# Normalizing the late attention runs through TensorE in a two-layer attention and mixer kernel

## The chip, the cores and the metric

The kernel runs on one core of one Trainium2 chip. The metric is the device time of one launch in microseconds (us). Times of several runs are given as a median; durations of single instructions come from one profiled execution.

The engines go by the profile's names: PE is TensorE (matmuls; PEld its weight loads), DVE is VectorE, ACT is ScalarE, POOL is GpSimd, SP is the engine whose queue issues most DMAs.

## The reference

Two blocks alternate, twice each, on x of 2048 tokens by 640 features (bf16 inputs):

```python
x = x + attention(layernorm(x), wqkv, wo)       # 32 heads of 20
x = x + token_mlp(layernorm(x), w1, b1, w2, b2) # over the 2048 tokens, 1536 hidden
x = x + attention(layernorm(x), wqkv, wo)
x = x + token_mlp(layernorm(x), w1, b1, w2, b2)

def attention(x, wqkv, wo):
    q, k, v = heads(x @ wqkv)
    p = softmax(q @ k.T * 20 ** -0.5)
    return merge(p @ v) @ wo

def token_mlp(x, w1, b1, w2, b2):      # x is normalized once more here
    u = gelu(layernorm(x).T @ w1 + b1)
    return (u @ w2 + b2).T
```

The scores are 32 x 2048 x 2048 per layer, so the work of attention is 134 million exponentials per layer.

## The kernel before, in words

**Attention.** Heads are taken four at a time (a group g of 8, each head padded to 32 partitions). A *unit* is one block of 512 queries (qb, four of them), one group and one tile of 128 keys (kt); it holds four *chunks* of 128 x 512 scores, one per head. For a chunk, PE makes S (128 keys x 512 queries, line L703), ACT turns three or two chunks at a time into P with one exponential (L773, 1536 or 1024 wide, alternating), and PE adds P times V into the accumulator `acc` (L1326). V has a column of ones per head, so row 20 of each head's 32 rows of `acc` is the softmax's sum. The sixteen units of one block and group are a *run*. In the last block of queries the units are 256 queries wide, and the last run is split in two halves.

Part of the chunks is not exponentiated on ACT but on DVE and POOL, in pairs, by integer and polynomial steps (L563, L661, L593, L597, L644, L614 or L616), from a PSUM bank `Dt` of their own into tiles `Pd`.

**Normalization of a run** (`finish_run`), all on DVE: `turn` transposes `acc` in 32 x 32 blocks into the f32 tile T1 (L810), so that queries come to lie on partitions; `recip` inverts the sums (L823); `scaled` multiplies (L826, into the bf16 tile T2); `back` transposes again into `attnT` (L834), which feeds the output projection. There is one accumulator bank: the next run's first product with V waits until `turn` has read it.

**Fills.** Everything else that PE does in attention is a *fill*, a short series of products into one PSUM bank (`misc`; early on also `Dt`), followed by an evacuation on DVE or ACT: the transposes of normalized tokens (T, L1225), projections to K and Q (L1177) and V (L1201), the output projection (O, L1117 and L1155), the first product of the mixer (M: six or eight products with `w1st`, L1068, added to the rows `ua` at L1076, whose weights come by DMA into two buffers), and in layer 1 the second product of layer 0's mixer (y, L1685).

**Order.** The order of all engines' work is written out while the program is built, by a planner that keeps a clock for each engine: `emit_S`, `emit_exp` and `emit_PV` lay out the main work, and `slot_work` puts fills into the gaps between the S products of two exponentials, in the order of a priority (`add_fill`). A fill's cost and its share of PE's activity are numbers that the caller states. [...] DVE's work is a list of `Proc`s, each with a rank and a list of steps with their costs. At the ramp of a layer, K and Q of the first groups are made as their tokens arrive: blocks of 512 tokens (tb), groups 0 to 3, for query blocks 0 and 1.

**End of a layer's attention.** After the last exponential, the planner runs what is left of the fills (`fill_step(tail_alloc)`) while the last run is normalized; `end_tiles` then makes the output projection of the last two token tiles in the S banks (L960), runs the remaining fills, whose evacuations are collected in `held`, and normalizes the two tiles: statistics (L980, `gather`), the rest (`spread`) and the apply steps (L995 on ACT, L999 on DVE). Then filler products keep PE going until the mixer's first products (`um`, L1753) of `mixer_head`. After layer 0 the mixer's head is followed by layer 1's ramp, after layer 1 by the mixer's tail (L1766, L1825).

Before the change the banks for these last fills are taken from a list of three:

```python
tail_banks = [sums[0][:, 1024:1536], None, None]

def tail_alloc():
    bank = tail_banks.pop()
    return bank if bank is not None else Dbank.alloc() if len(tail_banks) == 1 else misc.alloc()
```

At the very start, on DVE, the ones of V's extra column are set by a memset (L1546) among the statistics of the first token tiles.

Of the kernel before, what the change touches and what calls it, by code (L numbers as in the profile page):

```python
# [13 lines left out]
F32 = mybir.dt.float32  # L14
# [54 lines left out]

HOLD = 3  # L70
WARM_WAVES = 14
LOG2E = 1.4426950408889634
# [9 lines left out]
def kernel(  # L82
# [61 lines left out]
    ident = consts.tile([128, 128], BF16, name="ident")  # L144
    make_identity(nc, ident[:])
    mhalf = consts.tile([128, 1], F32, name="mhalf")
    nc.vector.memset(mhalf[:], -0.5)
# [76 lines left out]
    def attention(st, x_in_ap, x_mid, uacc_l, feed, feed_stack):  # L224
# [505 lines left out]
        def zeros(t):  # L730
            acc = runs[pv_run[0]]["acc"] if pv_run[0] < len(runs) else None
            if acc is not None:
                bank = acc
            elif not s_start:
                bank = warm_bank()
            elif late and fs["cur"] is not None and fs["idx"] > 0:
                zero_wave(fs["tile"], False, False, fs["cur"]["wave"], 512 if fs["cur"]["wave"] == WAVE else 320)
                return True
            elif fs["cur"] is None and misc.free <= pem["t"]:
                bank = misc.alloc()  # L740
            elif late and Dbank.free <= pem["t"]:
                bank = Dbank.alloc()
            elif t + 1 in S_tiles and pem["t"] + (0.0 if pem["mode"] == "S" else TURN) + PE_TO_ACT < exp_end.get(t, 0.0):
                for i, (n, j) in enumerate(tiles[t + 1]):
                    s_matmul(S_tiles[t + 1][:, i, :], n, j)
                s_start[t + 1] = pe_wave("S", cells=0.25 * len(tiles[t + 1]))
                return True
            else:
                return False
            zero_wave(bank, acc is None, acc is None)  # L750
            return True
# [39 lines left out]
        def finish_run(run):  # L791
# [8 lines left out]
            nth = part_no.get((qb, g), 0)  # L800
            whole = run["final"]
            if not whole:
                part_no[(qb, g)] = nth + 1

            def turn(end):
                if not whole and nth == 0:
                    box["T1"] = part_view((qb, g))
                else:
                    box["T1"] = ntmp.tile([128, 512], F32, name="T1")[:, c0:c1]
                nc.vector.transpose(out=box["T1"], in_=acc[:, c0:c1])  # L810
                acc_free[0] = end + DVE_TO_PE
# [16 lines left out]

            def back(end):
# [3 lines left out]
                to = attnT_tiles[qb][g]  # L833
                nc.vector.transpose(out=to[:, c0:c1], in_=T2[:, 0:nb, :].rearrange("p c i -> p (c i)"))  # L834

# [10 lines left out]
            rest = [(0.5, added, 0.0, True)] if nth else []  # L846
            if whole:
                rest += [(0.244, recip, 0.0), (0.15 + 0.34 * part, scaled, 0.0, True), (0.15 + 0.56 * part, back, 0.0)]
            ahead = [p for p in dvm["procs"] if getattr(p, "norm", False)]
            first = Proc(0, [(0.15 + 0.56 * part, turn, 0.0)], at + PE_TO_DVE)  # L850

            def turned(end):
                if rest:
                    p = Proc(norm_rank(run), rest, end + DVE_NEXT, after=after if whole else None,
                             allow=lambda me: not whole or (bool(late) and (len(me.steps) > 1 or at_live[0] < NG + 4)))
                    p.norm = True
                    submit(p)
            first.after = turned
            first.allow = lambda me: not any(p in dvm["procs"] for p in ahead)
            submit(first)  # L860

        early_left = set(early_runs)
        at_live = [0]
# [353 lines left out]
        def t_fill(tt, h_bf, ready, done):  # L1217
# [15 lines left out]
            def after(end):  # L1233
# [3 lines left out]
                if all(4 * tb + i in tready for i in range(4)):  # L1237
# [9 lines left out]
                    if tb in EQ and tb > 0:  # L1247
                        for g in range(EG):
                            proj_fill("Q", g, tb, base[tb] + 16.0 + 8.0 * g - 4, at, fed=True)
                if len(tready) == NT and NQB > 1:  # L1250
# [202 lines left out]
        for t in sums:  # L1453
            zero_wave(t[:, 0:512], True, True)
            zero_wave(t[:, 512:D], True, True, HALF / 2, D - 512)
        tail_banks = [sums[0][:, 1024:1536], None, None]

        def tail_alloc():
            bank = tail_banks.pop()
            return bank if bank is not None else Dbank.alloc() if len(tail_banks) == 1 else misc.alloc()  # L1460
        room = pem["t"] + 1.3
# [9 lines left out]
    class TokenFeed:  # L1471
        groups = 4
        early_qbs = (0, 1)
        ve_early = True
        act_helps = True
        act_free = 0.0
# [22 lines left out]
        def after_end(self, cx):  # L1499
            nc.gpsimd.memset(wo_pad[:], 0.0)  # L1500
            setup_wo()
            setup_biases()
# [3 lines left out]
        def begin(self, cx):  # L1506
# [376 lines left out]
```

## Time and profile before

| | |
|---|---|
| median of 3 runs | 1754.15 us (1754.06 to 1754.17) |
| the profiled execution's own time | 1754.05 us |
| its span, first to last instruction | 1752.3 us |
| mean granted TensorE clock | 1.000 |
| first exponential starts | 15.97 us |
| last exponential of layer 0 ends; first `um` product | 816.82; 823.27 us |
| first exponential of layer 1 starts | 853.26 us |
| last exponential of layer 1 ends; first `um` product | 1681.39; 1689.30 us |

A line of a group reads: source line, engine, operation, out<-in by tile names, shapes, count, then busy us, mean ns of one, then the engine's idle time just before them and what ended it. A line of a timeline reads: start, duration, engine, line, operation, count, and in brackets the idle time before it and what ended that. Line numbers are those of the kernel before.

### The profile page before, as it was taken

Reading aid. Unit: us, or ns where it says so; the run is one execution under the profiler, and the core shown is the slowest. Engines: PE = TensorE matmul, PEld = TensorE weight load, DVE = VectorE, ACT = ScalarE, POOL = GpSimd, SP = SyncE. Lnnn points to the kernel's source line nnn. Section 1 sums busy time; section 2 is a strip of 40 time slices with the busy share of each in tenths; the row PEclk is TensorE's granted clock in tenths of the full one; section 3 lists DMA queues with packets and bytes.
Section 4 is the critical chain, followed back from the end, with each engine's and each line's share of the span. In section 5 each row is a group of like instructions: output and inputs, shape, how many; then the busy total and the mean of one; then the engine's idle time right before and its main releaser. Section 6 shows DMA issues by size and latency. Waiting matters only on the chain.

```text
span 1752.3 us, 43289 instructions
## 1 busy us (share of the span) xinstructions
PE 1677.7 (96%) x17891; PEld 663.4 (38%) x17891; DVE 1534.9 (88%) x2491; ACT 1665.0 (95%) x1498; POOL 592.0 (34%) x936
## 2 busy tenths in 40 slices
PE   8999999999999999999999999999999999999999
PEld 3333333333333344444434433233333333444455
DVE  7789999999999999998543469999999999999973
ACT  8999999999999999999779999999999999999970
POOL 2243443353544343332000023434434443434310
PEclk9999999999999999999999999999999999999999
DMA  4020000000122010133322100001001220101445
GB/s 117 9 24 10 1 2 2 24 24 2 35 66 82 25 47 3 39 97 97 125 69 75 65 11 1 1 2 43 20 2 61 82 76 6 62 3 40 120 122 178
DMA packets 103014, 81.87 MB, mean 47 GB/s; under 512 B 50976, under 2 KB 87456, under 8 KB 102816
## 3 DMA queue, kind: packets, MB, share of 16 engines
q1 hardware_dynamic: 97280, 71.22, 13.5%
q0 software_dynamic: 5536, 7.88, 1.5%
q8 instruction: 140, 2.29, 0.5%
q14 instruction: 58, 0.48, 0.1%
HBM read 55.48 MB, written 23.59 MB: 45 GB/s over the span
## 4 chain that ended last, share of the span: by engine, by line
ACT 50%; PE 25%; issue 22%; DVE 2%; DMA 1%; POOL 0%; SPq 0%; ACTq 0%; DVEq 0%
ACT P L773 50%; PE S L703 7%; PE acc L1326 4%; PE misc L1068 2%; PE ya L1766 2%; PE misc L1177 2%; PE acc L762 2%; PE um L1753 1%; PE Dt L1177 1%; PE ya L1775 1%; PE yb L1766 1%; DMA w2s<-in_B_w_dram 1%; PE misc L1117 0%; PE misc L1685 0%; PE misc L1201 0%
## 5 line engine op out<-in xcount | busy, mean ns | idle before, releaser
L773 ACT ACTIVATE P<-S 128x1536 bf16<-128x1536 f32 (+1 forms) x1430 | 1617.4, 1369 | 13.5 <-PE S L703 13.0
L703 PE MATMUL S<-QTq,KT 32*128 32x512 bf16 (+1 forms) x4449 | 575.6, 337 | 60.9 <-ACT P L773 44.4
L661 POOL TENSOR_SCALAR ey<-ew 128x512 f16<-128x512 uint16 x516 | 320.6, 621 | 689.6 <-DVE et L597 306.4
L703 PEld LDWEIGHTS <-KT 32*128 32x128 bf16 x5127 | 229.6, 91 | 524.6 <-issue 497.0
L563 DVE TENSOR_SCALAR ew<-Dt 128x512 int32<-128x512 f32 x524 | 357.0, 681 | 22.3 <-PE Dt L703 14.8
L1326 PE MATMUL acc<-P,Vaug 128*32 128x512 bf16 (+1 forms) x4442 | 363.3, 343 | 0.3 <-DVE Vaug L370 0.3
L762 PE MATMUL acc<-zr,zw 128*32 128x512 bf16 x4256 | 328.1, 382 | 1.2 <-POOL zr L155 1.2
L597 DVE SCALAR_TENSOR_TENSOR et<-ey,ew 128x1024 int16<-128x1024 f16 x262 | 325.6, 1243 | 2.8
L644 POOL TENSOR_SCALAR Pd<-ew 128x512 int16<-128x512 int16 x317 | 196.8, 627 | 161.6 <-DVE et L597 42.4
L703 PE MATMUL Dt<-QTq,KT 32*128 32x512 bf16 (+1 forms) x678 | 201.4, 333 | 0.0
L593 DVE TENSOR_TENSOR ey<-ey 128x1024 f16<-128x1024 f16 x262 | 188.3, 719 | 1.4 <-POOL ey L661 0.3
L1326 PEld LDWEIGHTS <-Vaug 128*32 128x32 bf16 x5120 | 102.7, 94 | 175.4 <-issue 161.4
L762 PEld LDWEIGHTS <-zw 128*32 128x32 bf16 x4476 | 111.5, 96 | 97.9 <-issue 52.5
L616 DVE SCALAR_TENSOR_TENSOR Pd<-ew,et 128x1024 int16<-128x1024 int16 (+1 forms) x134 | 134.6, 1005 | 0.6
L614 DVE TENSOR_TENSOR Pd<-Pd,et 128x1024 int16<-128x1024 int16 (+1 forms) x189 | 121.8, 645 | 5.8 <-POOL Pd L644 3.8
L903 POOL TENSOR_TENSOR rstd<-veps,mhalf 128x1 f32<-128x1 f32 x60 | 49.4, 824 | 224.6 <-DVE veps L901 197.2
L1326 PE MATMUL acc<-Pd,Vaug 128*32 128x512 bf16 (+1 forms) x678 | 102.9, 336 | 1.4 <-DVE Pd L614 1.2
L1177 PE MATMUL misc<-hh,wq_pad 128*128 128x512 bf16 x290 | 84.0, 383 | 0.0
L1068 PEld LDWEIGHTS <-w1st 128*128 128x128 bf16 x672 | 52.9, 97 | 58.2 <-issue 45.3
L1177 PE MATMUL misc<-hh,wk_pad 128*128 128x512 bf16 x255 | 74.0, 383 | 0.0
L1068 PE MATMUL misc<-x1last,w1st 128*128 128x320 bf16 x384 | 73.0, 302 | 0.0
L1117 PE MATMUL misc<-wo_pad,attnT 128*128 128x320 bf16 x384 | 72.3, 302 | 0.2 <-DVE xin L1129 0.2
(145 smaller groups left out, 1180.4 us busy)
## 6 DMA issues: line engine op xcount, KB each, us to landing
w2s<-in_B_w_dram SPq DMA_DIRECT2D x16, 768.0 KB
uacc<-ustg POOLq DMA_DIRECT2D x24, 320.0 KB, 2.6
x1in<-xd SPq DMA_DIRECT2D x24, 320.0 KB
w1st<-in_B_w_dram SPq DMA_DIRECT2D x24, 256.0 KB
xd<-x2s SPq DMA_DIRECT2D x16, 320.0 KB
xin<-xd SPq DMA_DIRECT2D x16, 320.0 KB
w1st<-in_B_w_dram SPq DMA_DIRECT2D x24, 192.0 KB
xd<-x1s SPq DMA_DIRECT2D x12, 320.0 KB
```

The source lines that it names most:

```text
L563: nc.vector.tensor_scalar(out=w[:, slot, :], in0=Dt[:, :], scalar1=127.0 * FIX, scalar2=0.0, op0=ALU.add, op1=ALU.max)
L593: nc.vector.tensor_tensor(out=y, in0=y, in1=y, op=ALU.mult)
L597: nc.vector.scalar_tensor_tensor(out=box["t"][:, 0:512 * k], in0=ve_y.pop(p)[:, 0:512 * k], scalar=MANT_C * MANT_K ** 2, in1=frac, op0=ALU ...
L616: nc.vector.scalar_tensor_tensor(out=bits, in0=whole[:, lo:hi], scalar=128.0, in1=t, op0=ALU.mult, op1=ALU.add)
L644: after_vector(nc.gpsimd.tensor_scalar(out=bits, in0=whole, scalar1=128.0, scalar2=0.0, op0=ALU.mult, op1=ALU.add))
L661: return engine.tensor_scalar(out=out_ap, in0=in_ap, scalar1=MANT_K / FIX, scalar2=-MANT_K * MANT_S, op0=ALU.mult, op1=ALU.add)
L703: pe(nc.tensor.matmul(out_ap[:, c0:c0 + w], lhsT=KT[32 * j:32 * j + 32, g, kt * 128:(kt + 1) * 128], rhs=get_QT(st, qb)[32 * j:32 * j + 32 ...
L762: pe(nc.tensor.matmul(bank[32 * j:32 * j + 32, 0:w], lhsT=zw[:], rhs=zr[:, :, 0:64].to_broadcast([128, w // 64, 64]), start=start, stop=st ...
L773: nc.scalar.activation(out=P[:, 0:ncs, :].rearrange("p a b -> p (a b)"), in_=St[:, 0:ncs, :].rearrange("p a b -> p (a b)"), func=ACT.Exp, ...
L1068: pe(nc.tensor.matmul(t[:, 0:w], lhsT=w1_of[(p, ft)][:, sti, :], rhs=rows_in[sti][:, c0:c1], start=(sti == 0), stop=(sti == n_in - 1)))
L1177: pe(nc.tensor.matmul(t[:, :], lhsT=wpad[:, dt_, g, :], rhs=hT[:, dt_, tb * 512:(tb + 1) * 512], start=(dt_ == 0), stop=(dt_ == NDT - 1)))
L1326: pe(nc.tensor.matmul(acc[32 * j:32 * j + 32, a0:a0 + w], lhsT=Vaug[:, (kt * H + hh_) * VW:(kt * H + hh_) * VW + 32], rhs=P[:, slot, c0:c0 ...
```

## The change

Full-width runs of the second half of each layer (28 runs in all: those that close after unit 260, are not in parts, and are not among the last four) are normalized in another way. `turn` becomes a copy of `acc` to T1 without a transpose. Then two fills of a new kind, "N", follow through the bank `misc`, each of four steps: four f32 transposes of T1 on PE bring the sums into columns, and DVE inverts the sums out of PSUM; sixteen f32 products (32 columns each, four column tiles) of the inverted values with a f32 identity spread each value over its head's 32 rows, and one DVE product of this bank with T1 gives `attnT`. The next run's copy waits until both fills are done (`norm_open`). A f32 copy of the identity is made once, on POOL.

Further: in layer 1 the Q projections of the early query blocks after the first are queued ahead of the K projections of their tokens (`early_q`); the memset of V's ones is made due 3 us later in the plan; and the last fills of a layer may use the three banks in turn any number of times, for which the oldest held evacuation is put out before a bank is used again.

```diff
+NORM_SUMS = 0.3
+NORM_BACK = 0.3
+NORM_FROM = 260
+NORM_PRIO = 0.0
+NORM_OLD = 3
...
+            turned_over = whole and not nth and cursor[0] > NH * NORM_FROM and runs.index(run) < len(runs) - NORM_OLD
...
-                nc.vector.transpose(out=box["T1"], in_=acc[:, c0:c1])
+                if turned_over:
+                    nc.vector.tensor_copy(out=box["T1"], in_=acc[:, c0:c1])
+                else:
+                    nc.vector.transpose(out=box["T1"], in_=acc[:, c0:c1])
...
+            def chain():
+                nq = (c1 - c0) // 128
+                norm_open.append(run)
+
+                def sums_of(k):
+                    return lambda t: pe(nc.tensor.transpose(t[:, 128 * k:128 * k + 128],
+                                                            box["T1"][:, 128 * k:128 * k + 128], ident32[:]))
+
+                def inverse(t, end, eng):
+                    box["r"] = ntmp.tile([128, 16], F32, name="rden")
+                    nc.vector.reciprocal(out=box["r"][:, 0:4 * nq],
+                                         in_=t[:, 0:128 * nq].rearrange("p (c i) -> p c i", i=32)[:, :, DH])
+
+                def spread(end):
+                    def spread_of(k):
+                        def mm(t):
+                            for j in range(4):
+                                pe(nc.tensor.matmul(t[32 * j:32 * j + 32, 128 * k:128 * k + 128],
+                                                    lhsT=box["r"][:, 4 * k + j:4 * k + j + 1].to_broadcast([128, 32]), rhs=ident32[:],
+                                                    start=True, stop=True, skip_group_check=True, tile_position=(0, 32 * j)))
+                        return mm
+
+                    def scale(t, end, eng):
+                        nc.vector.tensor_tensor(out=attn_to(), in0=t[:, 0:128 * nq], in1=box["T1"], op=ALU.mult)
...
+                    add_fill(("N", qb, g, c0), cursor[0] / NH + NORM_PRIO, [spread_of(k) for k in range(nq)], scale, c1 - c0, ready=end + DVE_TO_PE,
+                             after=closed, wave=NORM_BACK, cells=0.5, gate=lambda: bool(late) and at_live[0] < NG + 4)
+                add_fill(("N", qb, g, c0), cursor[0] / NH + NORM_PRIO, [sums_of(k) for k in range(nq)], inverse, c1 - c0,
+                         ready=acc_free[0], after=spread, wave=NORM_SUMS, cells=0.5, cost=0.244)
...
-            if whole:
+            if whole and not turned_over:
...
-            first.allow = lambda me: not any(p in dvm["procs"] for p in ahead)
+            first.allow = lambda me: not norm_open and not any(p in dvm["procs"] for p in ahead)
...
-                            proj_fill("Q", g, tb, base[tb] + 16.0 + 8.0 * g - 4, at, fed=True)
+                            proj_fill("Q", g, tb, base[tb] + (8.0 * g + 12.0 if feed.early_q is None else 0.01 * g + feed.early_q),
+                                      at, fed=True)
...
-        tail_banks = [sums[0][:, 1024:1536], None, None]
+        tail_banks = [misc.alloc, Dbank.alloc, lambda: sums[0][:, 1024:1536]]
+        tail_used = [0]
 
         def tail_alloc():
-            bank = tail_banks.pop()
-            return bank if bank is not None else Dbank.alloc() if len(tail_banks) == 1 else misc.alloc()
+            if tail_used[0] >= len(tail_banks) and len(held) > 1:
+                force(held.pop(1))
+            tail_used[0] += 1
+            return tail_banks[(tail_used[0] - 1) % len(tail_banks)]()
...
+            nc.gpsimd.tensor_copy(out=ident32[:], in_=ident[:])
...
-                cx.submit(cx.Proc(2.6, [(0.49, lambda e: nc.vector.memset(Vv[:, :, :, DH:DH + 1], 1.0), 0.0)], e + 5.0))
+                cx.submit(cx.Proc(2.6, [(0.49, lambda e: nc.vector.memset(Vv[:, :, :, DH:DH + 1], 1.0), 0.0)], e + 8.0))
...
+        early_q = -5.5
```

More of the change, by code (lines that the diff above doesn't have):

```diff
@@ L145 @@
     make_identity(nc, ident[:])
+    ident32 = consts.tile([128, 128], F32, name="ident32")
     mhalf = consts.tile([128, 1], F32, name="mhalf")
@@ L735, in zeros @@
                 bank = warm_bank()
-            elif late and fs["cur"] is not None and fs["idx"] > 0:
+            elif late and fs["cur"] is not None and fs["idx"] > 0 and fs["cur"]["key"][0] != "N":
                 zero_wave(fs["tile"], False, False, fs["cur"]["wave"], 512 if fs["cur"]["wave"] == WAVE else 320)
@@ L827, in scaled, with attn_to @@
                                         in1=box["r"][:, 0:nb].unsqueeze(2).to_broadcast([128, nb, DH]), op=ALU.mult)
-            def back(end):
+            def attn_to():
                 if c0 == 0:
@@ L832, in back, with closed @@
                     at_live[0] += 1
-                to = attnT_tiles[qb][g]
-                nc.vector.transpose(out=to[:, c0:c1], in_=T2[:, 0:nb, :].rearrange("p c i -> p (c i)"))
+                return attnT_tiles[qb][g][:, c0:c1]
+            def back(end):
+                nc.vector.transpose(out=attn_to(), in_=T2[:, 0:nb, :].rearrange("p c i -> p (c i)"))
+            def chain():
[18 more added lines that the diff above has]
+                        nc.vector.tensor_tensor(out=attn_to(), in0=t[:, 0:128 * nq], in1=box["T1"], op=ALU.mult)
+                    def closed(end):
+                        norm_open.remove(run)
+                        after(end)
+                    add_fill(("N", qb, g, c0), cursor[0] / NH + NORM_PRIO, [spread_of(k) for k in range(nq)], scale, c1 - c0, ready=end + DVE_TO_PE,
+                             after=closed, wave=NORM_BACK, cells=0.5, gate=lambda: bool(late) and at_live[0] < NG + 4)
+                add_fill(("N", qb, g, c0), cursor[0] / NH + NORM_PRIO, [sums_of(k) for k in range(nq)], inverse, c1 - c0,
+                         ready=acc_free[0], after=spread, wave=NORM_SUMS, cells=0.5, cost=0.244)
             def after(end):
@@ L852, in turned @@
             def turned(end):
+                if turned_over:
+                    chain()
                 if rest:
@@ L858, in finish_run @@
             first.after = turned
-            first.allow = lambda me: not any(p in dvm["procs"] for p in ahead)
+            first.allow = lambda me: not norm_open and not any(p in dvm["procs"] for p in ahead)
             submit(first)
+        norm_open = []
         early_left = set(early_runs)
@@ L1474 @@
         ve_early = True
+        early_q = None
         act_helps = True
```

## The prediction

> **What bounds the kernel now.** I read the page's busy times first, then busy times by stretch, then the groups by line, and last the timelines at the three places where ScalarE stands still: the start, the ramp of layer 1, and the end of each layer's attention.
>
> ```profile
> PE 1677.7 (96%) x17891; PEld 663.4 (38%) x17891; DVE 1534.9 (88%) x2491; ACT 1665.0 (95%) x1498; POOL 592.0 (34%) x936
> ```
> ```profile
> 1200.00:1300.00 100.00, 95.66 (x939) 32.36 (x938) 98.23 (x154) 100.00 (x89) 42.70 (x66) 1.00 0.08 28
> 1300.00:1400.00 100.00, 95.88 (x852) 35.73 (x851) 97.61 (x158) 100.00 (x90) 44.66 (x72) 1.00 0.20 63
> ```
> Columns of the second view: stretch, its length, then busy time of PE, PEld, DVE, ACT, POOL, the granted clock, DMA. ACT, running exponentials, is 100% busy; PE has 4.2 us of idle in 100, DVE about 2; the clock is 1.00. Inside attention only ACT's own work counts.
>
> ```profile
> L773 ACT ACTIVATE P<-S 128x1536 bf16<-128x1536 f32 x714 | 1128.0, 1580 | 4.1 <-PE S L703 3.6 <-PE Dt L703 0.2
> L773 ACT ACTIVATE P<-S 128x1024 bf16<-128x1024 f32 x714 | 828.1, 1160 | 9.4 <-PE S L703 9.4
> ...
> L810 DVE STREAM_TRANSPOSE T<-acc 128x512 f32<-128x512 f32 x72 | 51.0, 708 | 9.5 <-PE acc L1326 9.1
> ...
> L834 DVE STREAM_TRANSPOSE attnT<-T 128x512 bf16<-128x512 bf16 x62 | 43.4, 700 | 0.0
> ```
> All exponentials together waited 13.5 us. Where, the ACT timeline shows; most of it is here, in layer 1's ramp:
> ```profile
> 853.26 21.84 ACT L773 ACTIVATE P<-S 128x1536 bf16<-128x1536 f32 x19 [0.43 <-PE S L703]
> 883.44 7.37 ACT L773 ACTIVATE P<-S 128x1024 bf16<-128x1024 f32 x7 [8.34 <-PE S L703]
> 892.16 7.38 ACT L773 ACTIVATE P<-S 128x1536 bf16<-128x1536 f32 x7 [1.35 <-PE S L703]
> 900.59 2.37 ACT L773 ACTIVATE P<-S 128x1024 bf16<-128x1024 f32 x2 [1.05 <-PE S L703]
> ```
> The end of attention is another regime: a chain PE - DVE - ACT. PE's, then DVE's timeline at the end of layer 1:
> ```profile
> 1682.33 0.72 PE L1068 MATMUL misc<-hh,w1st 128*128 128x320 bf16 x4
> 1683.85 0.97 PE L1068 MATMUL misc<-hh,w1st 128*128 128x320 bf16 x6 [0.81 <-DVE KT L1076]
> 1684.66 1.25 PE L960 MATMUL S<-wo_pad,attnT 128*128 128x512 bf16 x8
> 1685.75 0.98 PE L1068 MATMUL Dt<-hh,w1st 128*128 128x320 bf16 x6
> 1686.66 2.34 PE L762 MATMUL acc<-zr,zw 128*32 128x512 bf16 x40
> 1689.30 1.25 PE L1753 MATMUL um<-hh,KT 128*128 128x512 bf16 x8 [0.30 <-ACT hh L995]
> ```
> ```profile
> 1683.35 0.45 DVE L1076 TENSOR_TENSOR KT<-misc,KT 128x320 f32<-128x320 f32 x1
> 1684.87 0.49 DVE L1076 TENSOR_TENSOR KT<-misc,KT 128x320 f32<-128x320 f32 x1 [1.06 <-PE misc L1068]
> 1685.48 0.90 DVE L980 BATCH_NORM_STATS2 bnst<-S 128x6 f32<-128x320 f32 x2
> ```
> A leftover fill (six w1st products, L1068) holds PE 0.81 us (1683.85 to 1684.66); its add on DVE starts 1.02 us after its start and takes 0.48; the statistics come behind the adds; 3.82 us after the statistics start, the next layer's um products do. The last exponential, e, ended at 1681.39, so um starts at e+7.9. In layer 0 (e = 816.82, no fill left over) statistics start at 819.45 and um at 823.27: again 3.82 apart, and e+6.45.
>
> **The change part by part.** Counts come from the instructions of the two programs as built.
>
> *DVE and ACT.* 28 of the 62 full-width normalizations change form. Out go 0.708 + 0.242 + 0.552 + 0.700 = 2.20 us of DVE each (L810, L823, L826, L834); in come a copy (as L370's 128x512 cast, 0.685), the same reciprocal, and a product with a PSUM operand (as L372, 0.682): 1.61. DVE gains 28 x 0.59 = 16.5 us. The planner spends it: 10 more chunks of exponentials go to DVE, five pairs at 2 x 0.681 + 0.719 + 1.243 + about 1.0 = 4.3 us. So DVE stays as full, and ACT loses two 1536-wide and two 1024-wide exponentials, one of each per layer. 602 of them take 681.48 us in the timeline, 2.26 us for two: **-4.5 us**, on the path.
>
> *PE in the late runs.* Each of the 28 runs gets four f32 transposes and four steps of four 32-row f32 products; 1188 filler products (L762) go. No f32 product is in the trace. Lower end: as bf16 128-wide transposes (L1225, five in 0.45 us, the last 0.22: 0.057 each), 8 x 0.057 = 0.5 us a run. Upper end: every sum at a whole 512-wide record (0.383), every spread product at a whole 128-wide one (0.219), nothing overlapping: 5.0 us. The plan reserves 8 x 0.3 = 2.4. A run lasts 24.5 us, in which PE has about 1.05 us of idle. I take 2.6 us, about midway between the ends: 0.2 over the plan, covered by the idle but for **+0.6 us** in all; without that cover 0.2 x 28 = 5.6. The upper end is 2.6 over the plan and leaves (2.6 - 1.05) x 28 = 43 us on the path, the lower nothing, as PE is not the bound. New wait: an open chain holds back the next run's copy out of acc, and behind it that run's first PV product on PE; but a chain spans some seven exponentials (8 us) of a run's 24.5.
>
> [...]
>
> *Start.* The memset of V's ones column moves behind eight DVE instructions. It starts at 10.06 after 1.90 us of DVE idle, with the h_bf of the fourth tile behind it at 10.14; that tile's rstd is done at 8.79. If the idle goes with the memset, the h_bf starts at 8.85 and the first exponential (15.97) up to 1.2 us earlier; if it belongs to the place, 0.1. Middle: **-0.6**.
>
> *Layer 1's second queries first.* PE's order up to the second gap is unchanged, so the 8.34 us (the fourth group's K and Q stand behind 72 y products) stay. The Q product takes the K product's place, PE meets S about 0.2 earlier, and then sixteen units are open at once instead of four, so the 1.05 goes: **-1.25** (between -0.8 and -2.4).
>
> *End of the layers.* Each late chain holds the bank misc twice, so the w1st fills that share it come later: 8 are left in layer 0 (one partly done), 6 in layer 1, against 0 and 3. Layer 0, in time after e: the first ends, its add waits for the last normalization, PE resumes at 2.46 (as in layer 1 above), fill to 3.27, fill to 4.08, wo_pad products to 5.17, then fills. The new bank rotation forces the adds of the four oldest before DVE's statistics. Those fills start at 5.17, 5.98, 6.79 and 7.60; but the last pair's weights use a buffer released only at 5.98. The first x load at the start is used 1.9 us after its issue ended; with 0.37 for the issue the weights land at 8.25, the add runs 9.27 to 9.75, statistics at 9.7, um at 13.5: **+7.1** (+6.4 with the weights in time, +8 with a slower load). Layer 1: the two fills behind wo_pad (ends 4.36) start at 4.36 and 5.17, add 6.19 to 6.67, um at 10.4: **+2.5**. The fewer fillers there (40 instead of 56, 24 instead of 40) end before um; the w2s loads fall behind the wv load, but are needed 3.06 us after um only. The one copy of the identity on POOL (34% busy) costs nothing.
>
> Sum: -4.5 + 0.6 - 0.6 - 1.25 + 7.1 + 2.5 = +3.85. The profiled execution took 1754.05 (span 1752.3), 0.1 under the median of 1754.15: 1758.0.
>
> **The rivals.**
>
> *The f32 steps are dear.* For it: no row prices them, and PE has only 4% idle. Against: the zero waves (L762) show four column tiles side by side, 0.22 us for four of 512. Midway into the open range, 3.6 to 4.4 us a run against 2.4, less 1.05, gives 4 to 27 us more: about 1770.
>
> [...]
>
> *The end costs little (faster).* The leftover fills would cost nothing if PE stood waiting at e for other reasons, or if the plan leaves them but the chip runs PE ahead and finishes them before e. Place: the adds before the statistics; price 9.6 us; without it 1758.0 - 9.6 = 1748.4. The change is faster than before once less than 5.7 of the 9.6 is paid. Against: layer 1's rows above show the same queue paid in full for fewer fills, and PE has no spare time before e.
>
> **How the numbers follow.** About 0.2% (3.5 us) is what a measurement of this kernel can tell from no change; 1757.7 is the mark above. The forecast case (1755.5 to 1760.5) has 0.60, half on each side of it; dear steps 0.17 and the clock 0.05, both slower; the cheap end 0.18, of which 0.12 below 1750.6. So slower 0.30 + 0.22 = 0.52, same 0.30 + 0.06 = 0.36, faster 0.12. The forecast case's own range is 1755.5 to 1760.5; for 8 in 10 I take 1750 to 1769, leaving out the best of the cheap end and the dearest steps.
>
> **What would show it.** Right: 1426 exponentials, ACT still at 100% in late stretches; um of layer 0 some 13 us after the last exponential, of layer 1 some 10; the 8.34 us gap still there, the 1.05 gone. Wrong: S products that ACT waits for in late runs (dear steps), a clock under 1.00, or statistics that start as early after e as before.

## The result, and the profile after

The changed kernel takes 1767.66 us, median of 5 runs (1766.31 to 1770.09), against 1754.15 (1754.06 to 1755.25): 13.5 us slower, ratio 1.0079, 95% interval [1.0068, 1.0090]. Its profiled execution took 1770.09, with a span of 1768.0 and a mean granted clock of 0.995; the span before was 1752.3 at 1.000. Line numbers are now those of the changed kernel.

Busy times of the page, then by stretch (the same columns as before the change):

```profile
PE 1667.4 (94%) x17740; PEld 681.4 (39%) x17740; DVE 1547.2 (88%) x2505; ACT 1661.5 (94%) x1494; POOL 601.3 (34%) x960
```
```profile
1200.00:1300.00 100.00, 95.27 (x967) 33.36 (x966) 97.86 (x151) 99.84 (x89) 43.49 (x68) 1.00 0.08 28
1300.00:1400.00 100.00, 94.40 (x890) 34.53 (x887) 96.62 (x153) 99.59 (x89) 45.56 (x73) 0.98 0.12 37
1500.00:1600.00 100.00, 93.77 (x1468) 44.23 (x1470) 92.40 (x145) 95.68 (x85) 39.26 (x59) 0.93 0.11 34
```

DVE and POOL did some more, PE and ACT some less, and ACT's 100% is gone in one stretch: 95.68 between 1500 and 1600 (99.98 before), where the clock is 0.93. The exponentials and the parts of the new normalization, by shape:

```profile
L779 ACT ACTIVATE P<-S 128x1536 bf16<-128x1536 f32 x712 | 1120.8, 1574 | 12.6 <-PE S L709 11.1 <-PE Dt L709 0.8 <-PE acc L1375 0.2
L779 ACT ACTIVATE P<-S 128x1024 bf16<-128x1024 f32 x712 | 821.6, 1154 | 8.5 <-PE S L709 8.3
...
L818 DVE COPY T<-acc 128x512 f32<-128x512 f32 x28 | 19.1, 683 | 0.4 <-PE acc L1375 0.2
L871 DVE TENSOR_TENSOR attnT<-misc,T 128x512 bf16<-128x512 f32 x28 | 19.1, 682 | 0.2
```

The counts over both layers are those of the forecast, and the copy (683 ns) and the product (682 ns) cost DVE what the neighbouring rows said. The exponentials waited 21.1 us instead of 13.5. Where the span grew, the ACT and PE timelines show (from the first exponential of a layer to its last, then to the first `um`; times in us):

| stretch | before | after | difference |
|---|---|---|---|
| start to first exponential | 15.97 | 17.64 | +1.67 |
| layer 0's exponentials | 800.85 | 799.75 | -1.10 |
| last exponential to `um`, layer 0 | 6.45 | 15.57 | +9.12 |
| `um` to first exponential of layer 1 | 29.99 | 30.00 | 0.0 |
| layer 1's exponentials | 828.14 | 830.69 | +2.55 |
| last exponential to `um`, layer 1 | 7.90 | 11.34 | +3.44 |
| `um` to the end | 63.0 | 63.0 | 0.0 |

These add up to the 15.7 us between the two spans; the profiled execution is the slowest of the five, 2.4 us above the median. The end of layer 0 is the largest item. PE, then DVE there (the last exponential ended at 817.39):

```profile
821.57 1.25 PE L1008 MATMUL S<-wo_pad,attnT 128*128 128x512 bf16 x8
822.65 0.98 PE L1116 MATMUL S<-hh,w1st 128*128 128x320 bf16 x6
823.88 0.99 PE L1116 MATMUL misc<-hh,w1st 128*128 128x320 bf16 x6 [0.25 <-DMA w1st<-in_B_w_dram]
824.71 0.98 PE L1116 MATMUL Dt<-hh,w1st 128*128 128x320 bf16 x6
827.73 0.99 PE L1116 MATMUL S<-hh,w1st 128*128 128x320 bf16 x6 [2.04 <-DMA w1st<-in_B_w_dram]
828.56 0.98 PE L1116 MATMUL misc<-hh,w1st 128*128 128x320 bf16 x6
829.47 2.34 PE L768 MATMUL acc<-zr,zw 128*32 128x512 bf16 x40
832.96 1.25 PE L1808 MATMUL um<-hh,KT 128*128 128x512 bf16 x8 [1.16 <-ACT hh L1043]
```
```profile
828.76 0.49 DVE L1124 TENSOR_TENSOR KT<-S,KT 128x320 f32<-128x320 f32 x1 [2.54 <-PE S L1116]
829.17 0.89 DVE L1028 BATCH_NORM_STATS2 bnst<-S 128x6 f32<-128x320 f32 x2
```

The leftover w1st fills (L1116) run one behind the other, the last row of weights comes 2.04 us late, the add (L1124) waits 2.54 us for that, and the statistics (L1028) stand behind that add. The statistics start at 829.17, and `um` 3.79 us later.

At the start, DVE and PE:

```profile
14.23 0.48 DVE L1600 MEMSET Vaug<- 128x512 bf16 x1 [1.87 <-ACT wq_pad L1613]
14.33 0.70 DVE L376 CAST Vaug<-misc 128x320 bf16<-128x320 f32 x1
```
```profile
15.09 1.24 PE L1225 MATMUL misc<-hh,wq_pad 128*128 128x512 bf16 x5 [2.77 <-DVE Vaug L376]
```

The memset kept the idle time before it (1.90 us at its old place, 1.87 here). Behind it stands now the evacuation of V (L376) out of the bank `misc`, and PE waits 2.77 us for that bank with the Q products that the first exponential needs.

Layer 1's ramp on ACT, then what is new in its late runs:

```profile
862.96 21.84 ACT L779 ACTIVATE P<-S 128x1536 bf16<-128x1536 f32 x19 [0.43 <-PE S L709]
893.13 7.37 ACT L779 ACTIVATE P<-S 128x1024 bf16<-128x1024 f32 x7 [8.34 <-PE S L709]
901.71 310.36 ACT L779 ACTIVATE P<-S 128x1536 bf16<-128x1536 f32 x274 [1.21 <-PE S L709]
...
1505.59 2.54 ACT L779 ACTIVATE P<-S 128x1536 bf16<-128x1536 f32 x2 [0.68 <-PE S L709]
1509.69 2.36 ACT L779 ACTIVATE P<-S 128x1536 bf16<-128x1536 f32 x2 [1.56 <-PE S L709]
1512.62 2.54 ACT L779 ACTIVATE P<-S 128x1536 bf16<-128x1536 f32 x2 [0.57 <-PE S L709]
1516.54 177.11 ACT L779 ACTIVATE P<-S 128x1536 bf16<-128x1536 f32 x157 [1.38 <-PE S L709]
```

The 8.34 stays, 1.35 became 1.21, the 1.05 is gone; 4.2 us of stalls between 1505 and 1517 are new. There the granted clock (third column from the end) falls:

```profile
1499.20:1502.60 3.40, 2.65 (x51) 1.60 (x50) 3.37 (x6) 3.40 (x5) 0.61 (x1) 0.97 0.30 109
1502.60:1506.00 3.40, 3.40 (x44) 1.48 (x40) 2.72 (x5) 2.72 (x4) 1.78 (x3) 0.50 0.00 0
1506.00:1509.40 3.40, 3.40 (x38) 1.19 (x30) 2.45 (x3) 2.06 (x2) 0.69 (x2) 0.50 0.00 0
```

A chain of layer 1 runs at 1499 to 1504. A second, shorter dip, of some 3.5 us, is at the first chain of layer 1 (1328 to 1332, mean clock 0.57) and costs ACT 0.2 us. The dips differ between executions: those at a mean clock of 0.995 took 1770.0 to 1770.1 us, that at 0.997 took 1767.7, those at 0.998 and 0.999 took 1766.3 and 1766.7. So one long dip is worth some 3.5 us, by these five executions. In the kernels below, too, the times spread over a few us, and the slower executions are mostly those with a lower mean clock (with the memset back: 1756.5 and 1756.8 at 1.000, 1759.5 and 1760.1 at 0.998).

### The profile page after: what moved, and what is told of

Same layout as the page of the kernel before. It is cut to its first block, busy times and chain, and to the rows that moved or that the text cites. A ratio compares the mean times of both kernels' runs of the same rounds, so it can differ in the third digit from the quotient of the medians.

```text
span 1768.0 us, 43047 instructions
## 1 busy us (share of the span) xinstructions
PE 1667.4 (94%) x17740; PEld 681.4 (39%) x17740; DVE 1547.2 (88%) x2505; ACT 1661.5 (94%) x1494; POOL 601.3 (34%) x960
## 3 DMA queue, kind: packets, MB, share of 16 engines
q1 hardware_dynamic: 97280, 71.22, 13.6%
q0 software_dynamic: 5536, 7.88, 1.4%
## 4 chain that ended last, share of the span: by engine, by line
ACT 53%; issue 23%; PE 21%; DVE 2%; DMA 1%; SPq 0%; POOL 0%; ACTq 0%; DVEq 0%
ACT P L779 52%; PE S L709 6%; PE acc L1375 3%; PE ya L1821 2%; PE misc L1225 2%; PE misc L1116 1%; PE acc L768 1%; PE misc L1165 1%; PE um L1808 1%; PE ya L1830 1%; PE yb L1821 1%; PE Dt L1740 0%; DMA w1st<-in_B_w_dram 0%; PE misc L1740 0%; PE Dt L1225 0%
## 5 line engine op out<-in xcount | busy, mean ns | idle before, releaser
L709 PE MATMUL S<-QTq,KT 32*128 32x512 bf16 (+1 forms) x4466 | 581.6, 338 | 79.8 <-ACT P L779 57.9
L709 PEld LDWEIGHTS <-KT 32*128 32x128 bf16 x5156 | 237.1, 91 | 524.0 <-issue 485.6
L569 DVE TENSOR_SCALAR ew<-Dt 128x512 int32<-128x512 f32 x534 | 363.7, 681 | 25.2 <-PE Dt L709 16.9
L1375 PE MATMUL acc<-P,Vaug 128*32 128x512 bf16 (+1 forms) x4430 | 355.7, 344 | 0.0
L603 DVE SCALAR_TENSOR_TENSOR et<-ey,ew 128x1024 int16<-128x1024 f16 x267 | 335.0, 1255 | 2.8
L650 POOL TENSOR_SCALAR Pd<-ew 128x512 int16<-128x512 int16 x332 | 204.1, 619 | 158.0 <-DVE ey L599 46.1
L768 PE MATMUL acc<-zr,zw 128*32 128x512 bf16 x3096 | 245.2, 383 | 1.2 <-POOL zr L161 1.2
L620 DVE TENSOR_TENSOR Pd<-Pd,et 128x1024 int16<-128x1024 int16 (+1 forms) x202 | 128.7, 637 | 7.7 <-POOL Pd L650 4.9
L768 PEld LDWEIGHTS <-zw 128*32 128x32 bf16 x3288 | 82.1, 96 | 73.2 <-issue 40.2
L1225 PE MATMUL misc<-hh,wk_pad 128*128 128x512 bf16 x275 | 79.6, 383 | 0.0
L1116 PEld LDWEIGHTS <-w1st 128*128 128x128 bf16 x672 | 53.2, 97 | 59.7 <-issue 41.0
L1116 PE MATMUL misc<-x1last,w1st 128*128 128x320 bf16 x384 | 71.4, 302 | 0.0
```

Source lines behind the costliest of these rows:

```text
L569: nc.vector.tensor_scalar(out=w[:, slot, :], in0=Dt[:, :], scalar1=127.0 * FIX, scalar2=0.0, op0=ALU.add, op1=ALU.max)
L603: nc.vector.scalar_tensor_tensor(out=box["t"][:, 0:512 * k], in0=ve_y.pop(p)[:, 0:512 * k], scalar=MANT_C * MANT_K ** 2, in1=frac, op0=ALU ...
L650: after_vector(nc.gpsimd.tensor_scalar(out=bits, in0=whole, scalar1=128.0, scalar2=0.0, op0=ALU.mult, op1=ALU.add))
L709: pe(nc.tensor.matmul(out_ap[:, c0:c0 + w], lhsT=KT[32 * j:32 * j + 32, g, kt * 128:(kt + 1) * 128], rhs=get_QT(st, qb)[32 * j:32 * j + 32 ...
L768: pe(nc.tensor.matmul(bank[32 * j:32 * j + 32, 0:w], lhsT=zw[:], rhs=zr[:, :, 0:64].to_broadcast([128, w // 64, 64]), start=start, stop=st ...
L1116: pe(nc.tensor.matmul(t[:, 0:w], lhsT=w1_of[(p, ft)][:, sti, :], rhs=rows_in[sti][:, c0:c1], start=(sti == 0), stop=(sti == n_in - 1)))
```

## The experiments

**The chains off.**

```diff
-NORM_FROM = 260
+NORM_FROM = 10 ** 6
```


> All 62 runs are normalized on DVE as before; the later memset, layer 1's early Q and the new bank rotation stay. Theory 1 (the time is lost outside attention, by the start and by fills that the chains leave over): first exponential still at 17.6 (+1.7 against before), um of layer 0 back at e+6.5 (no w1st product is left over there), um of layer 1 at e+9 (30 products left over, 19 before, 37 after), layer 1's ramp 1.2 shorter, two exponentials fewer than before (-2.3), clock 1.000: about 1753.5 to 1755. Theory 2 (the loss is of the start, ramp or bank rotation and not of the chains): stays near 1766.

Measured: 1758.34 us (1756.81 to 1759.67), ratio to before 1.0022 [1.0013, 1.0031]. Some 9 of the 13.5 us go with the chains, not all. In its profile layer 0's end is 6.43, layer 1's attention 826.06, but the first exponential starts at 19.02, and `um` of layer 1 at e+10.62. The start is even later than in the run above, and there the clock fell while PE stood idle for 1.53 of 3.40 us (first row): PE was busy for 1.87 us with six records, in the same stretch of the change, at 1.00, for 1.91 us with ten:

```profile
13.60:17.00 3.40, 1.87 (x6) 0.76 (x6) 2.25 (x6) 0.00 (x0) 0.55 (x1) 0.78 0.13 30
17.00:20.40 3.40, 3.40 (x17) 1.13 (x15) 1.58 (x3) 1.38 (x2) 0.00 (x0) 0.72 0.88 216
```

Theory 1 had the places right; it priced the start (at 17.6) and layer 1's end (at e+9) too low. The late start differs by execution: the profiles of the five kernels with the late memset have it at 17.36 to 19.02, and only those from 18.2 on have the clock fall there (to between 0.69 and 0.81, from 13.6 to 20.4). Two exponentials fewer in layer 1 (721 against 723), and 30 leftover products at its end, come without a single chain; by their widths, though, that is only two chunks less for ACT.

**The memset back.**

```diff
-... nc.vector.memset(Vv[:, :, :, DH:DH + 1], 1.0), 0.0)], e + 8.0))
+... nc.vector.memset(Vv[:, :, :, DH:DH + 1], 1.0), 0.0)], e + 5.0))
```


> Only the due time of the ones memset goes back (e + 8.0 to e + 5.0). Theory 1 (the 1.9 us of DVE idle belongs to the memset itself and goes where it goes): first exponential back at 16.0, -1.7; layer 0 has 40 leftover w1st products in place of 48, -0.8: about 1763 to 1765, clock dips aside. Theory 2 (the late start is another part's): first exponential stays at 17.6, no gain.

Measured: 1758.33 us (1756.46 to 1760.12), 9.3 below the change with one number put back. The first exponential is at 16.01, as expected; the time fell by far more than expected. The rest is the plan's: with another start it lays out everything behind differently. `um` of layer 0 comes at e+10.51, not +15.57, as 40 products are left over for 48 and no fill waits there for its weights any more; the stalls at 1505 are gone, and so are three stalls of ACT in layer 0 (0.61, 0.78 and 0.42 us, at 135 to 232), which the kernels with the late memset share. So the memset's move cost far more than its own 1.9 us, through what the plan made of the rest. The 9.3 us here and the 9.3 of the run without chains can't be parts of one sum, as together they exceed the 13.5.

**The statistics ahead of the leftover fills.**

```diff
-            held.append(None)
-            while fs["cur"] is not None or fill_queue:
-                fill_step(alloc)
-            ...
             gather(0)
             ...
             spread(1)
+            held.append(None)
+            while fs["cur"] is not None or fill_queue:
+                fill_step(alloc)
+            ...
```


> The leftover fills behind the wo_pad products are issued after the statistics and the apply steps of the first of the last two tiles, not before them. Theory 1 (the forced adds hold back the statistics): um of layer 0 from e+15.6 to about e+12.2, where the last fill ends on PE, um of layer 1 from e+11.4 to about e+10: together 4 to 5 us less, 1762 to 1763. Theory 2 (the late weights of the fills set um, the statistics are hidden): um within 0.5 of where it was, no gain.

Measured: 1765.82 us (1765.31 to 1767.67); `um` of layer 0 at e+15.02, of layer 1 at e+11.56. Theory 2, about: the statistics now start early (823.78, e+5.0), and it gains layer 0's end only 0.55 us and layer 1's nothing, as the fills themselves are late, one through weights (1.67 us), and `um` comes behind them on PE. The profile lacks the long dip of the clock (it has a short one, 0.53 from 1329 to 1333), so the 1.8 us between the medians is not a gain of the ends:

```profile
825.53 0.97 PE L1115 MATMUL S<-hh,w1st 128*128 128x320 bf16 x6 [1.31 <-ACT x1last L1023]
...
829.80 0.99 PE L1115 MATMUL S<-hh,w1st 128*128 128x320 bf16 x6 [1.67 <-DMA w1st<-in_B_w_dram]
...
831.53 2.34 PE L768 MATMUL acc<-zr,zw 128*32 128x512 bf16 x40
833.81 1.26 PE L1807 MATMUL um<-hh,KT 128*128 128x512 bf16 x7
```

The edit has a price of its own (1.31 us of PE, waiting for the copy out of the shared S bank), so it bounds what the order of the adds is worth, no more.

**Half of the w1 loads left out.**

```diff
+            if p == len(M_GROUPS) - 1 and ft % 2 and ft < NF:
+                w1_of[(p, ft)] = w1_of[(p, ft - 1)]
             if ft < NF and (p, ft) not in w1_of:
```


> The changed kernel, but in the last group of w1st products every second row of weights is not loaded: its products use the weights of the row before (so the mixer's sums are of other weights). Theory 1 (the leftover fills at the ends wait for weights: 2.04 + 0.25 us of PE idle in layer 0, 1.97 in layer 1): um of layer 0 from e+15.6 to about e+13.3, of layer 1 from e+11.3 to e+10.5, 3 us less in all: 1763 to 1765. Theory 2 (the adds before the statistics alone set um, the loads are hidden): no gain, 1767.

Measured: 1762.59 us (1760.93 to 1766.48), 5.1 below the change; `um` of layer 0 at e+12.92, of layer 1 at e+10.54. Theory 1, to 0.4 us in both places; the time is 0.4 under its range. No leftover fill waits for weights now, so the rest of layer 0's gap to e+6.45 is left to the fills themselves and their adds.

**The plan's price of a step.**

```diff
-NORM_SUMS = 0.3
-NORM_BACK = 0.3
+NORM_SUMS = 0.2
+NORM_BACK = 0.22
```


> The plan's price of a step of a chain goes from 0.3 to the measured 0.20 (a f32 transpose) and 0.22 (four spread products). The program gets 316 more filler products, and 5 and 6 fewer leftover w1st products in the two layers. Theory 1 (the clock falls where a chain leaves too little work on PE): clock 1.000 in every execution, the 4.2 us of stalls between 1505 and 1517 gone, and the ends 0.8 each shorter: 1762 to 1764. Theory 2 (f32 steps do not count as work, whatever is around them): granted clock still 0.995 to 0.999, 1764 to 1768. Theory 3 (f32 steps are dear): more stalls, above 1768.

Measured: 1763.85 us (1763.01 to 1766.15), clock 0.998 to 0.999. The stalls at 1505 are gone and the time is as theory 1 had it, but not its parts. The clock is not 1.000: in the profile it dips elsewhere, at layer 0's end (0.86 from 827.2, 0.64 from 830.6 to 834.0). And the ends are not each 0.8 shorter: `um` comes at e+11.07, 4.5 earlier, and, with 31 leftover products, at e+12.93, 1.6 later: there PE waits 2.63 us for the weights of the fourth fill. So the match in time is partly luck, and the run doesn't decide between theories 1 and 2. Theory 3 is out.

**Every f32 step twice** (on the kernel with the memset back).

```diff
-                    return lambda t: pe(nc.tensor.transpose(...))
+                    return lambda t: [pe(nc.tensor.transpose(...)) for _ in range(2)]
...
-                            for j in range(4):
+                            for j in (0, 1, 2, 3, 0, 1, 2, 3):
```


> As with the memset back, and every f32 step of the chains is issued twice (the same transposes and products into the same places), which the plan does not know of. Theory 1 (a step of four spread products takes 0.22 us and a transpose 0.1 to 0.2, and PE's spare time in a run hides them): some 1.4 us more PE work in each of 28 runs, against 1 to 2 us of idle and filler: 0 to 10 us above the 1758.3 of the run with the memset back. Theory 2 (f32 steps are dear and already on the path): 28 x 2.6, 1800 and more. Theory 3 (f32 steps do not count for the clock): stretches at half the clock in the late runs, 20 us and more.

Measured: 1764.63 us (1763.46 to 1765.54), 6.3 above the 1758.33 with single steps. The steps' groups with single steps (the kernel with the memset back), then doubled:

```profile
L865 PE MATMUL misc<-ident,rden 128*32 128x128 f32 x896 | 37.9, 279 | 0.0
L853 PE MATMUL misc<-ident,T 128*128 128x128 f32 x112 | 26.9, 306 | 0.0
```
```profile
L865 PE MATMUL misc<-ident,rden 128*32 128x128 f32 x1792 | 62.3, 276 | 0.0
L853 PE MATMUL misc<-ident,T 128*128 128x128 f32 x224 | 39.1, 289 | 0.0
```

36.6 us more of PE work, 1.31 a run, lengthened the two layers' exponentials by 3.42 + 1.92 = 5.34, 0.19 a run. PE's spare time hides most of even a second set, and the first set cost nothing that can be seen: with single steps layer 0's exponentials have no gap left in ACT's timeline. Theory 1. The clock of this profile is 1.000, and 0.999 to 1.000 in all executions: theory 3 is out in its strong form.

**Early Q alone** (chains off and memset back: both edits shown above).

> Chains off and the memset back at its place: of the change only layer 1's early Q and the bank rotation are left. Theory 1 (in the run without chains the early Q took 2.1 us out of layer 1's attention, and the late memset made the start 3.05 longer): first exponential at 16.0, layer 0 as before (800.9, um at e+6.5), layer 1's attention 826.1 (-2.1), um of layer 1 at e+9 to e+10.6 (30 leftover w1st products against 19): 1753 to 1755. Theory 2 (the 4 us of the run without chains come from elsewhere): 1757 and more.

Measured: 1755.36 us (1755.28 to 1756.70), ratio 1.0006 [0.9998, 1.0015]: no difference that can be told. First exponential 16.02, layer 0 800.86, layer 1 826.60 (-1.54), `um` of layer 1 at e+10.63 (+2.73). Theory 1, 0.4 us above its range. What layer 1's attention wins, its end takes back and more, where 30 products are left over against 19. Without the chains and the late memset, then, 1.2 of the 13.5 us remain.

Between this kernel and the one with the memset back lie the 28 chains alone, and they cost 3.0 us: -1.83 in layer 0's exponentials, -0.52 in layer 1's, +4.06 at layer 0's end, +0.62 behind it, +0.83 at layer 1's end (spans: +3.2). The late memset alone costs 3.0 us too (the run without chains, 1758.34). Both together cost 12.3, so 6.3 us appear only where both are: in the change's profile layer 0's waits for weights (2.3 us) and the long dip of the clock (4.2 us of stalls) are of this kind, as neither has them in its profile.

**Fewer chains** (14; memset back).

```diff
-NORM_OLD = 3
+NORM_OLD = 10
```


> The last eleven runs of a layer, not four, stay without a chain (14 chains, not 28), and the memset is at its old place. Nothing is left over at the end of layer 0, and 16 w1st products at the end of layer 1 (19 before). Theory 1 (the chains cost by the fills that they leave over at the end, and give 1.8 us in layer 0): um of layer 0 at e+6.5 and of layer 1 at e+8, layer 1's attention 826.1: 1751 to 1753, faster than before. Theory 2 (each chain costs in its run): half way between 1758.3 and the run without chains.

Measured: 1751.07 us (1750.14 to 1752.26), ratio 0.9980 [0.9971, 0.9989]: faster than both kernels, by 3.1 us than the one before. `um` comes at e+6.42 and e+7.20, layer 1's exponentials take 825.55. Theory 1 has the time, but not the gain of 1.8 in layer 0 (800.72 for 800.85). Against the kernel before, the span is 3.0 shorter by layer 1: 2.59 in its exponentials and 0.70 at its end. Against the early Q alone, which has most of the first too (826.60), the largest item is layer 1's end, e+7.20 for e+10.63, with 16 products left over for 30. So what pays is how little is left over there; why the plan leaves less with 14 chains than with none stays open.

**The memset on POOL**, in the change, in the kernel with 14 chains, with 22 (`NORM_OLD = 6`), and in the kernel before (the edit is shown in the change).

```diff
-                cx.submit(cx.Proc(2.6, [(0.49, lambda e: nc.vector.memset(Vv[:, :, :, DH:DH + 1], 1.0), 0.0)], ...))
+                nc.gpsimd.memset(Vv[:, :, :, DH:DH + 1], 1.0)
```


> The ones are set by POOL, right behind ACT's zeros, not by DVE. All else as in the change. Theory 1 (the 1.9 us of idle belong to DVE's memset): no such idle on DVE in the first 16 us, first exponential 1 to 2 us earlier than with the memset at its old place, that is 14 to 15 against 16.0: 1756 to 1757.5 against 1758.3. Theory 2 (the start is bound by the loads of tokens or weights): first exponential at 16.0, 1758.3.

> Fourteen chains as in the run of half the chains (1751.1), and the ones set by POOL. By the run with POOL's memset the first exponential starts 1.07 us earlier, the rest is as there (no leftover products in layer 0, 16 in layer 1): 1750.0. Rival (an earlier start is lost again in layer 0's ramp): 1751.

> As the last, but only the last seven runs of a layer are without a chain (22 chains); 18 and 26 leftover w1st products at the ends of the layers. If the leftover products set the price: layer 0's end about e+7.5, layer 1's about e+9.5, one exponential fewer in layer 0: 1751 to 1753, above the kernel with 14 chains. If the chains' gain grows with their number: under 1750.

> The kernel before, with the ones set by POOL behind ACT's zeros; nothing else. Theory 1: the first exponential goes from 16.0 to 14.9, all else keeps its length: 1753.1. Rival: lost again in the ramp, 1754.2.

Measured: 1757.06 (1756.41 to 1760.35), 1750.59 (1749.43 to 1751.51; ratio 0.9979 [0.9970, 0.9988]), 1753.57 (1752.19 to 1756.09; 0.9995 [0.9986, 1.0004]) and 1753.78 us (1753.17 to 1755.72; 0.9999 [0.9990, 1.0007]). The memset on POOL, in the change:

```profile
3.28 2.47 POOL L1600 MEMSET Vaug<- 128x512 bf16 x1 [0.68 <-ACT Vaug L1598]
```

It takes 2.47 us there, about as much as idle time and record together on DVE (1.87 + 0.48 in the change, 1.90 + 0.48 before). As that idle time moved with the instruction and is gone without it, it was most likely the instruction itself. DVE no longer stands still for it, but the first exponential is at 14.94, 16.09, 15.12 and 15.97: in two of the four profiles the next tokens landed a us later and DVE waited for them instead. In the kernel before:

```profile
10.59 0.49 DVE L886 BATCH_NORM_STATS2 bnst<-x0in 128x6 f32<-128x320 bf16 x1 [1.08 <-DMA x0in<-in_A_x_dram]
```

So about the expected 1.07 us came in two executions of four, and neither theory holds alone; by the medians it is 0.4 to 1.3. The lowest median of all is the second's, 3.6 us under the kernel before; its executions overlap with those of the 14 chains and DVE's memset. The third, with 18 and 26 leftover products, missed its range by 0.6 on the slow side; its profile has dips at both first chains (0.54 from 454.4 to 457.8, 0.61 from 1319.0 to 1322.4) and behind layer 1's end (0.78 and 0.72, from 1688.4 to 1695.2).

Leftover products (counted in the programs as built) and the time from the last exponential to `um`, over the profiled executions: in layer 0, 0 or 3 products 6.4 to 6.5 us, 18: 7.88, 40: 10.5, 43: 11.07, 48: 15.0 and 15.6 (12.9 with half the loads); in layer 1, 16: 7.2, 19: 7.9, 26: 10.15, 30: 10.6, 31: 12.9, 37: 11.1 to 11.6 (10.5 with half the loads). The time grows with the number, though not evenly; at 48, at 31 and at 37 PE's waits for late weights are added, 1.5 to 2.6 us of them.

## Why the prediction was right or wrong

The forecast was slower, in a range of 1750 to 1769. The time of 1767.66 is slower and inside, but the forecast case itself, 1755.5 to 1760.5, missed it by 7. The mechanism of the largest term, fills left over at the end of layer 0, was right. That the time lies inside the range is partly luck: the range's upper end was set by dear f32 steps, which the runs refute, and what filled it were other things.

Term by term, in the spans: the start +1.67 for -0.6, the exponentials of both layers +1.45 for -5.15 (-4.5 + 0.6 - 1.25), layer 0's end +9.12 for +7.1, layer 1's end +3.44 for +2.5. Of the 11.8 us that the spans moved beyond the forecast, the exponentials have 6.6, of which 4.4 are the stalls in the two dips of the clock and 1.5 those of layer 0 that go with the late memset. And the sum took its terms as independent, where 6.3 of the 13.5 us come from the chains and the late memset only together. By its steps:

**DVE and ACT.** The count (1426 exponentials) and DVE's prices were right; "one of each per layer" was not: layer 0 lost two 1536-wide ones, layer 1 two 1024-wide ones. How many chunks went to DVE, its first step on each shows; in order the kernel before, the change, the run without chains, and early Q alone:

```profile
L563 DVE TENSOR_SCALAR ew<-Dt 128x512 int32<-128x512 f32 x524 | 357.0, 681 | 22.3 <-PE Dt L703 14.8
L569 DVE TENSOR_SCALAR ew<-Dt 128x512 int32<-128x512 f32 x534 | 363.7, 681 | 25.2 <-PE Dt L709 16.9
L569 DVE TENSOR_SCALAR ew<-Dt 128x512 int32<-128x512 f32 x528 | 359.8, 681 | 21.1 <-PE Dt L709 14.2
L569 DVE TENSOR_SCALAR ew<-Dt 128x512 int32<-128x512 f32 x526 | 358.2, 681 | 23.8 <-PE Dt L709 16.7
```

So the chains account for six of the ten chunks (528 to 534; 526 to 532 with the memset back), and the planner did spend most of what they freed (three pairs at 4.3 us, of 16.5). They won 2.35 us of both layers' time together (the memset back against early Q alone), where six tenths of the 4.5 would be 2.7. The four other chunks come with the late start and early Q, and layer 1's exponentials in early Q alone took only 0.4 us less of ACT's time than before. In the change the stalls took back more than the whole gain.

**PE in the late runs.** Taken at 2.6 us a run; the records with the memset back give (37.9 + 26.9) / 28 = 2.31. The cost on the path, +0.6, was nothing that can be seen, the dips apart. Four spread products make eight records; twelve in a row took 0.86 us and four 0.42 (in the change, at 459.28 and 460.82), so each further step of four took 0.22. The rival of dear steps is refuted by doubling them.

**Start.** Forecast -0.6, measured +1.67: the sign was wrong. The h_bf of the fourth tile did start early (8.95 against the 8.85 of the step). It brought little: the next statistics waited 0.98 us for their tokens (10.38, against 10.61 before). What failed is that the term counted only what the memset would leave, not what it would now precede: the evacuation of V, and the bank `misc`, for which the first Q products wait.

**Layer 1's second queries first.** Forecast -1.25, measured in the ramp's gaps -1.19. The 8.34 stayed, as said.

**End of layer 0.** Forecast e+13.5, measured e+15.57; mechanism and order were right, the weights' term was mis-sized. I let them land 2.27 us after their buffer was free. By SP's timeline, the loads issued at 820.95 and 823.66 were used at 823.88 and 827.73: 2.9 and 4.1 us. With half of these loads away `um` came at e+12.92. That the adds hold back the statistics is true, but with the statistics first the fills themselves were nearly as late (e+15.02).

**End of layer 1.** Forecast e+10.4, measured e+11.34, for another reason in part. The statistics started at 1700.40, e+6.75, near the e+6.6 that the forecast amounts to, but `um` came 4.6 us after them and not 3.8, as it stood behind late fills on PE:

```profile
1701.85 0.99 PE L1116 MATMUL misc<-hh,w1st 128*128 128x320 bf16 x6 [1.97 <-DMA w1st<-in_B_w_dram]
1702.67 0.98 PE L1116 MATMUL Dt<-hh,w1st 128*128 128x320 bf16 x6
1703.58 1.48 PE L768 MATMUL acc<-zr,zw 128*32 128x512 bf16 x24
1704.99 1.26 PE L1808 MATMUL um<-hh,KT 128*128 128x512 bf16 x8
```

With half of the loads away it was e+10.54, again 3.8 us after the statistics. And 30 of the 37 products are left over without any chain, by the plan that follows the early Q.

**The clock.** That it falls was given 0.05. No run shows a fall at every one of the 28 chains, or what that would cost. It did fall, in the profiled execution, at two of them (to 0.50 and 0.57), and the long dip cost ACT 4.2 us: the rival was half true. One pattern stands ahead of both, of the dip with 14 chains and of layer 1's with 22: three f32 transposes in a row, then PE idle until ACT leaves the S bank (at 1498.52 in the change, at 453.49 with 14 chains, 0.64 from 456.8 to 460.2, and at 1315.85 with 22, 0.61 from 1319.0 to 1322.4), as here at 1325.85:

```profile
1325.85 0.55 PE L853 MATMUL misc<-ident,T 128*128 128x128 f32 x3
1326.87 0.59 PE L709 MATMUL S<-QTq,KT 32*128 32x512 bf16 x3 [0.48 <-ACT P L779]
1327.39 0.33 PE L853 MATMUL misc<-ident,T 128*128 128x128 f32 x1
```

But the pattern alone does not make a dip: eight chains of the change have it and two dipped, thirteen have it with the memset back and none dipped in its profile, issuing each transpose twice (three more of 0.11 us, by estimate most of the idle time) brought no dip either, and other dips came with waits alone, at the start (0.78 and 0.72 in the run without chains) and at layer 0's end (0.64 with the plan's lower prices). How much of it is the transposes and how much the 0.47 us of idle time stays open.

**The cheap end** (1748.4) is refuted for the change as it is; the nearest to it that was run, with 14 chains, the memset back and nothing left over in layer 0, took 1751.07.

## What to carry to other kernels

Where a plan lays out all engines, a change that frees one engine can be paid for, as here, at the places where the plan empties its queues: count what is left over at the end of each stage in the built program, and price the loads that stand behind it by the latency from issue to use (2.9 and 4.1 us here), not by the transfer of an idle queue. Move an instruction only after asking what it will then precede, as well as what it leaves. Count a price in the unit that moves: four exponentials fewer were ten chunks, and their number alone hid which part of the change had moved them. A PE that is 96% busy had room here for 2.3 us of work in 24.5, as its fillers gave way.

## What the runs showed of the hardware

- A memset of 512 two-byte values per partition, 48 bytes apart, took 2.47 us on POOL (in the change with POOL's memset). On DVE the profile shows 0.48 us of it and 1.9 us of idle time before, at both places where it stood (10.06 before, 14.23 in the change).
- Once the granted clock had fallen to 0.50, it stayed there for some 13.6 us (1502.6 to 1516.2 in the change; 0.52 in the last quarter), although PE's records show it busy throughout, 13.60 of 13.60 us. Why it stayed is open.
- A step of four f32 products of 32 columns in four column tiles took 0.22 us in a row (twelve products 0.86 at 459.28, four 0.42 at 460.82, in the change), and f32 transposes of 128 x 128 0.11 each (three 0.55 at 1325.85, one 0.33 at 1327.39).
- The changed kernel had a mean clock of 0.995 in two executions and 0.998 or 0.999 in two others, 3.5 us apart; the kernel before stayed at 1.000 or 0.999 in all its runs, 1754.05 to 1755.80.
